# A product of spectra moved from VectorE to ScalarE and GpSimd, a bias given as an immediate, and two loads issued at other places

## The chip, the cores and the metric

The kernel runs on one core of a Trainium2 chip. The core has a matrix engine (TensorE, PE in the profile; its weight loads are shown apart as PEld), a vector engine (VectorE, DVE), an activation engine (ScalarE, ACT), a general engine (GpSimd, POOL) and a queue that only issues DMAs (SyncE, SP; ACT and POOL have DMA queues too). Each engine works its own instructions in order; semaphores make one wait for another. The matrix engine writes its results into PSUM, which GpSimd can't read in this kernel; everything else lies in SBUF, with DRAM behind it. The metric is the device time of one execution in microseconds (us); lower is better.

## The reference: what is computed

One input u of 2048 rows and 448 columns goes through two branches, and a gate per row mixes their outputs.

```python
g = _sigmoid((x * gate_w).sum(-1, keepdims=True))
a = _A_ref(x, ...)      # a long convolution
b = _B_ref(x, ...)      # attention in 4 segments with a memory
return g * a + (1 - g) * b
```

The convolution's filter is a sum of decaying oscillations, and the convolution is done by Fourier transforms of twice the length:

```python
P = jnp.exp((A * dt[:, None])[:, :, None] * pos[None, None, :])
K = 2.0 * jnp.einsum("dn,dnl->dl", C, P).real
Kf = jnp.fft.rfft(K, L2)
Uf = jnp.fft.rfft(u_t, L2)
y = jnp.fft.irfft(Uf * Kf[None, :, :], L2)[:, :, :L]
```

Its product `Uf * Kf` is the "product of spectra" of the title. The filter needs cosines and sines of 448 x 256 phases over the positions. The attention has 16 heads of 28 columns and 4 segments of 512 rows: within a segment a causal softmax, across segments a linear memory with a normalisation.

## The kernel before

The program has two halves.

The first half (to about 448 us) builds the filter, projects u to queries, keys and values, and does the first step of the Fourier transform of u. `first_half` goes through 56 steps n. In each, TensorE builds the phases in PSUM (`turns`), ScalarE makes from them, in `trig`, a sine straight from PSUM, an absolute value straight from PSUM, and a cosine in place in SBUF (a Sin with a bias of pi/2 and a negative scale), VectorE multiplies them with exponentials (`product`, lines 393 to 399), and TensorE sums them (`sums`). Between these steps `Feed` hands out pieces of the projections by a list of costs. In this half the order on VectorE and ScalarE is the program's own: `k.act`, `k.copy` and `k.vector` tie each instruction behind the one before it on its engine. The bias of the cosine is a tile of one column, `k.bhp`, filled once with pi/2; it is also the bias of one cosine in `prepare_params`.

The second half (`second_half`) holds the attention and the convolution. The attention works in 16 units (four segments times four groups of four heads). For each unit `maxima` does the scores of the row maxima (TensorE into `ps_a`, VectorE's masked maximum into `jk` and `mx`, line 992) and puts the negated maxima into the unit's query tile by a small DMA of POOL's queue (line 1004). `weigh` does the scores again with the maxima included, ScalarE takes the exponential into `PT` (line 1023), POOL masks it (line 1034). `values` multiplies with the values (`ps_pv`). At the end of a segment, `seg_end` normalises, recalls the memory and projects out; parts of that pass through DMAs of POOL's queue (lines 1067, 1068, 1098) and products on POOL (`skip`, line 1121).

The convolution (`convolve`) works in 32 chunks c. `transform` multiplies a chunk of the filter, `gk`, and ScalarE copies the result from PSUM into `ks` (line 599). `product` multiplies a chunk of u, `gu`, and VectorE multiplies the result in PSUM with `ks` into `pr` (line 604). `back` takes two finished chunks of `pr` through the first step back; ScalarE copies that into `bs` (line 617) and stores it. `pr` and `ks` have three buffers each. Each resumption of `convolve` does one of these steps; the loop over the units resumes it 1.15 times in each of the six rounds of a unit, from unit 1 to unit 12. At an odd c the order is: transform(c), product(c - 1), back(c - 3), which reads `pr` of c - 3 and c - 2.

The PSUM of the second half has three double banks of the tag `a`. The scores of both kinds, transform, product and back all take them in turn, so that an engine that is late to empty one holds TensorE. TensorE's own instructions are in program order (`k.mm`, `k.tr`). On ScalarE, VectorE and POOL in this half most instructions are placed by the planner of the framework, which orders what it can by its own estimates; the products of `skip` are held in program order.

Before the units start, `transform_k` does eight steps that turn the filter into `GK` in DRAM; each writes one store of 896 KB. In the same loop (`for r in range(8)`) the rounds of `maxima` of unit 0, and in the end the first of unit 1, are taken. Loads of a unit's q and k (`load`, 512 KB each, four buffers) are issued on SP's queue: unit 0 before the loop, unit 1 at r = 1, unit 2 after the loop and after the first loads of the convolution have been asked for, unit i + 3 at the start of unit i. SP's order is held by marks: `k.mark(x)` makes every later `k.dma` issue behind x. Each GK store is marked, and so is the load of k of the first three units. `k.ldma` also issues behind the latest load of a chunk of u (`k.late`); among the units' loads only unit 3 uses it.

Of the kernel before, what the change touches and what calls it, by code (L numbers as in the profile page):

```python
# [12 lines left out]
F32 = mybir.dt.float32  # L13
# [3 lines left out]
AF = mybir.ActivationFunctionType  # L17
ALU = mybir.AluOpType
# [5 lines left out]
D = 448  # L24
# [7 lines left out]
TWO_PI = 2 * math.pi  # L32
# [112 lines left out]
def accurate_exp(v, pool, x, P, W):  # L145


    def t(tag, dt=F32):
        return pool.tile([P, W], dt, tag=tag, name=tag)

    n, r, p = t("ee_n"), t("ee_r"), t("ee_p")
    a, b = t("ee_a"), t("ee_b")
    ia, ib = t("ee_ia", I32), t("ee_ib", I32)
    v.tensor_scalar(n, x, 1.0 / math.log(2.0), MAG, ALU.mult, ALU.add)
    v.tensor_scalar(n, n, MAG, -250.0, ALU.subtract, ALU.max)
    v.tensor_scalar(n, n, 250.0, None, ALU.min)
    c1 = 0.693359375
    c2 = math.log(2.0) - c1
    v.scalar_tensor_tensor(r, n, -c1, x, ALU.mult, ALU.add)
    v.scalar_tensor_tensor(r, n, -c2, r, ALU.mult, ALU.add)  # L160
    co = [1.0 / math.factorial(i) for i in range(9)]
    v.tensor_scalar(p, r, co[8], co[7], ALU.mult, ALU.add)
    for i in range(6, -1, -1):
        v.tensor_tensor(p, p, r, ALU.mult)
        v.tensor_scalar(p, p, co[i], None, ALU.add)
    v.tensor_scalar(a, n, 0.5, MAG, ALU.mult, ALU.add)
    v.tensor_scalar(a, a, MAG, None, ALU.subtract)
    v.tensor_tensor(b, n, a, ALU.subtract)
    for f, i in ((a, ia), (b, ib)):
        v.tensor_scalar(f, f, 127.0, 8388608.0, ALU.add, ALU.mult)  # L170
        v.tensor_copy(i, f)
    v.tensor_tensor(p, p, ia.bitcast(F32), ALU.mult)
    v.tensor_tensor(p, p, ib.bitcast(F32), ALU.mult)
    return p
# [3 lines left out]
def prepare_params(nc, k, pool, early, gp):  # L178

    ld = pool.tile([112, 4], F32, name="ld")
    nc.sync.dma_start(ld, k.log_dt.rearrange("(j p) -> p j", p=112))
    W = [112, 4, N]

    def new(nm, where=pool):
        return where.tile(W, F32, name="pin_" + nm)

    def load(nm, src, where=pool):
        t = new(nm, where)
        nc.sync.dma_start(t, src.rearrange("(j p) n -> p j n", p=112))
        return t

    cr = load("cr", k.C_real)
    ci = load("ci", k.C_imag)
    la = load("la", k.log_A_real)
    ai = load("ai", k.A_imag)
    k.ident = k.cp.tile([128, 128], F32, name="ident")  # L200
    nc.sync.dma_start(k.ident, k.c_id)
    k.ce = gp.tile([128, 3, 512], BF16, name="ce")
    nc.sync.dma_start(k.ce, k.c_ce)


    last = {}

    def chain(e, op, *args, **kw):
        if e in last:
            with k.issue_after(last[e].ins):  # L210
                x = op(*args, **kw)
        else:
            x = op(*args, **kw)
        last[e] = x

    class Chained:
        def __getattr__(self, name):
            return functools.partial(chain, "v", getattr(nc.vector, name))

    v = Chained()  # L220
    act = functools.partial(chain, "a", nc.scalar.activation)
    stt, tt, ts = v.scalar_tensor_tensor, v.tensor_tensor, v.tensor_scalar

    def wide(x):
        return x.unsqueeze(2).broadcast_to(W)

    def parts(w, t, sub, queue):
        for s in range(3):
            sp = pool.tile(W, BF16, tag="sp", name="sp", bufs=3)
            k.copy(sp, t, AF.Copy)  # L230
            if s < 2:
                sub(t, t, sp, ALU.subtract)
            queue(w[:, :, s], sp)
            yield

    b, c = new("b", early), new("c", early)
    mx, mn = new("mx", early), new("mn", early)
    f, g, e = (new(n, early) for n in "fge")
    a, d = new("a"), new("d")
    dt = accurate_exp(v, pool, ld, 112, 4)  # L240
    dtp = pool.tile([112, 4], F32, name="dtp")
    dt2 = pool.tile([112, 4], F32, name="dt2")

    act(b, cr, AF.Abs)
    act(c, ci, AF.Abs)
    act(la, la, AF.Exp)
    stt(mx, b, 1e-37, c, ALU.max, ALU.max)
    ts(dtp, dt, 1.0 / TWO_PI, None, ALU.mult)
    ts(dt2, dt, 2.0, None, ALU.mult)
    v.reciprocal(f, mx)  # L250
    yield 4
    nc.gpsimd.tensor_tensor(la, la, wide(dt), ALU.mult)
    for _ in parts(k.SD, la, nc.gpsimd.tensor_tensor, k.pdma):
        pass
    tt(mn, b, c, ALU.min)
    tt(f, f, mn, ALU.mult)
    act(g, f, AF.Arctan)
    yield 4
    yield "decays"
    tt(d, c, b, ALU.is_gt)  # L260

    tt(ai, ai, wide(dtp), ALU.mult)
    ts(e, ai, MAG, None, ALU.add)
    stt(a, e, MAG, ai, ALU.subtract, ALU.subtract)
    ts(d, d, 0.25, None, ALU.mult)

    stt(d, g, 1.0 / TWO_PI, d, ALU.mult, ALU.subtract)
    nc.scalar.activation(d, d, AF.Abs)
    ts(cr, cr, 0.0, 0.5, ALU.is_lt, ALU.mult)
    ts(ai, a, 32.0, None, ALU.mult)  # L270
    ts(e, ai, MAG, None, ALU.add)
    stt(ai, e, MAG, ai, ALU.subtract, ALU.subtract)
    tt(cr, d, cr, ALU.subtract)
    nc.scalar.activation(cr, cr, AF.Abs)
    stt(ai, a, 0.5, ai, ALU.mult, ALU.add)
    ts(ci, ci, 0.0, -2.0, ALU.is_lt, ALU.mult)
    ts(ci, ci, 1.0, None, ALU.add)
    yield 2
    tt(ci, cr, ci, ALU.mult)

    tt(ci, ci, ai, ALU.add)
    ts(e, ci, MAG, None, ALU.add)
    stt(d, e, MAG, ci, ALU.subtract, ALU.subtract)
    pa, pd = parts(k.SP[:, :, 0], a, tt, k.adma), parts(k.SP[:, :, 1], d, tt, k.adma)
    for s in range(3):
        for x in (pa, pd):
            next(x)
        yield 1
    act(c, g, AF.Sin, bias=k.bhp[:112], scale=-1.0)
    act(b, g, AF.Sin)  # L290
    yield "phases"
    yield 2
    tt(mx, mx, c, ALU.mult)
    tt(mn, mn, b, ALU.mult)
    tt(mx, mx, mn, ALU.add)
    tt(mx, mx, wide(dt2), ALU.mult)
    yield 4
    for nt in range(2):
        pt = k.ps("m")
        for j in range(4):  # L300
            k.tr(
                pt[:, 112 * j : 112 * j + 112], mx[:, j, 128 * nt : 128 * nt + 128], k.ident[:112, :112]
            )
        v.tensor_copy(
            k.cab[:, nt].rearrange("n (p j) -> n j p", j=4), pt[:, :D].rearrange("n (j p) -> n j p", j=4)
        )


def first_half(nc, k, gy, feed):
# [4 lines left out]
    act, v = k.act, nc.vector  # L314
# [61 lines left out]
    def trig(n):  # L376

        pt = arg.pop(n)
        cs[n] = t = gw.tile([128, 2, 2, 2, 256], F32, tag="cs", name="cs", bufs=2)
        pv = pt.rearrange("p t (w c) -> p t w c", w=2)  # L380
        act(t[:, 1].rearrange("p w t c -> p t w c"), pv, AF.Sin, scale=TWO_PI)
        act(t[:, 0].rearrange("p w t c -> p t w c"), pv, AF.Abs)
        fl = t[:, 0].rearrange("p w t c -> p (w t c)")
        act(fl, fl, AF.Sin, bias=k.bhp, scale=-TWO_PI)

    def product(n):
        J, c = divmod(n, 2)
# [179 lines left out]
def convolve(nc, k, fp):  # L567
# [3 lines left out]
    cf, cb, gk, gu, ks, pr = {}, {}, {}, {}, {}, {}  # L571
# [29 lines left out]
    def product(c):  # L601
        pt = second(c, gu.pop(c), 0)
        pr[c] = fp.tile([128, 2, D], F32, tag="pr", name="pr", bufs=3)
        nc.vector.tensor_tensor(pr[c], pt, ks.pop(c), ALU.mult)  # L604

    def back(c):

# [328 lines left out]
def attend(nc, k, ap):  # L936
# [15 lines left out]
    def load(i):  # L952
        if i >= 16:
            return
        s, hg = divmod(i, 4)
        queue = k.ldma if i == 3 else k.dma
        for t, T, src in (("q", Q, k.QD), ("k", K, k.KD)):
            T[i] = ap.tile([128, 2, SEG], F32R, tag=t, name=t + "u", bufs=4)
            x = queue(T[i].bitcast(F32), src[s, hg])
        if i < 3:  # L960
            k.mark(x)

# [242 lines left out]
def second_half(nc, k, ap, tp, fp, fin):  # L1205
# [5 lines left out]
    def step(g):  # L1211
        return next(g, none) is not none
# [16 lines left out]
    for r in range(8):  # L1229
        step(first)  # L1230
        if r == 1:
            k.load(1)
        for _ in range((0, 1, 2, 1, 2, 1, 1, 0)[r]):
            step(ms[0])
        if r >= 6:
            step(ms[1])
# [9 lines left out]
    fp = fp()  # L1246
    cv = convolve(nc, k, fp)
    step(cv)
    k.load(2)
    vals = k.values(0)  # L1250
    step(vals)
    for r in range(4):
# [72 lines left out]
def gated_mix(ctx, tc, k):  # L1325
    nc = tc.nc
# [14 lines left out]
    def act(*args, **kw):  # L1341
        if k.strict:
            return follow("act", nc.scalar.activation, *args, **kw)
        return tc.keep_in_program_order(nc.scalar.activation(*args, **kw))
# [124 lines left out]

    k.gates = gates  # L1470

    k.bhp = cp.tile([128, 1], F32, name="bhp")
    nc.vector.memset(k.bhp, math.pi / 2)

    def turn_over(pt, n):


# [134 lines left out]
```

## Time and profile before

| | |
|---|---|
| median of 3 runs | 866.55 us (866.17 to 876.26) |
| span of the profiled execution | 866.7 us |
| mean granted TensorE clock | 0.942 |
| busy: PE, PEld, DVE | 753.7, 410.3, 596.9 us |
| busy: ACT, POOL | 539.2, 173.1 us |
| DMA: moved, mean rate | 153.11 MB, 177 GB/s |

The profile is of one execution, whose span is the time from its first to its last instruction. Busy times count what an engine executes; PE's and PEld's overlap. Rows of a group read: line, engine, operation, output and inputs with their shapes, count, then the busy time in us and the mean of one in ns, and after the second bar the idle time of the engine just before these instructions, with what ended it. Rows of a timeline or of the chain begin with the start and the length in us. The clock is a share of full speed. Lines such as 1335, 1356, 1370, 1384 and 1386 are those of helpers (`follow`, `copy`, `mm`, `dma`), so tiles tell more than lines there.

### The profile page before, as it was taken

Reading aid. Unit: us, or ns where it says so; the run is one execution under the profiler, and the core shown is the slowest. Engines: PE = TensorE matmul, PEld = TensorE weight load, DVE = VectorE, ACT = ScalarE, POOL = GpSimd, SP = SyncE. Lnnn points to the kernel's source line nnn. Section 1 sums busy time; section 2 is a strip of 40 time slices with the busy share of each in tenths; the row PEclk is TensorE's granted clock in tenths of the full one; section 3 lists DMA queues with packets and bytes.
Section 4 is the critical chain, followed back from the end, with each engine's and each line's share of the span. In section 5 each row is a group of like instructions: output and inputs, shape, how many; then the busy total and the mean of one; then the engine's idle time right before and its main releaser. Section 6 shows DMA issues by size and latency. Waiting matters only on the chain.

```text
span 866.7 us, 18996 instructions
## 1 busy us (share of the span) xinstructions
PE 753.7 (87%) x7575; PEld 410.3 (47%) x7597; DVE 596.9 (69%) x1160; ACT 539.2 (62%) x638; POOL 173.1 (20%) x217
## 2 busy tenths in 40 slices
PE   1687988998879988799979799999997998888997
PEld 1364655765547644476534444444443443343443
DVE  7988778777787777877648656656664747664564
ACT  4876989798997999979842255544453434431220
POOL 5224111001110011101100111222313124222110
PEclk9998999998999999999979689999999999878799
DMA  9347753334633255323569948557465545654873
GB/s 242 91 110 247 227 185 104 96 111 154 205 124 96 96 169 194 122 92 132 178 218 347 317 133 264 178 193 249 139 222 189 193 162 168 216 187 164 221 231 100
DMA packets 88290, 153.11 MB, mean 177 GB/s; under 512 B 20626, under 2 KB 57162, under 8 KB 88154
## 3 DMA queue, kind: packets, MB, share of 16 engines
q1 hardware_dynamic: 79130, 140.83, 50.2%
q10 hardware_dynamic: 7424, 9.18, 3.1%
q0 software_dynamic: 1648, 1.89, 0.7%
q8 instruction: 60, 0.98, 0.5%
q14 instruction: 28, 0.23, 0.1%
HBM read 90.87 MB, written 60.63 MB: 175 GB/s over the span
## 4 chain that ended last, share of the span: by engine, by line
PE 52%; ACT 16%; DVE 13%; issue 7%; DMA 7%; POOL 2%; SPq 1%; ACTq 0%; DVEq 0%; POOLq 0%
PE ps_a L1370 18%; PE ps_m L1370 16%; PE ps_pv L1370 7%; ACT cs L1335 7%; PE ps_arg L1370 4%; DVE jk L992 3%; PE ps_k L1370 3%; PE ps_m L1373 2%; ACT L1335 2%; DVE Y L397 2%; DMA WD<-wsp 1%; ACT EX L1335 1%; DMA dn<-pvs 1%; DVE Y L398 1%; DMA ident<-in_c_id 1%
## 5 line engine op out<-in xcount | busy, mean ns | idle before, releaser
L1023 ACT ACTIVATE PT<-ps_a 128x1024 f32<-128x1024 f32 (+1 forms) x96 | 84.5, 881 | 122.9 <-PE ps_a L1370 115.9
L992 DVE CUSTOM_DVE_ANT_0 jk<-ps_a,mk 128x512 f32<-128x512 f32 (+3 forms) x256 | 124.9, 488 | 49.6 <-PE ps_a L1370 42.3
L359 POOL TENSOR_TENSOR EX<-EX,cab 128x1024 f32<-128x1024 f32 x28 | 54.0, 1928 | 309.3 <-ACT EX L1335 286.3
L1335 ACT ACTIVATE cs<-ps_arg 128x1024 f32<-128x1024 f32 x111 | 107.3, 1021 | 2.7 <-DVE Y L398 2.4
L1370 PE MATMUL ps_a<-qu,ku 32*128 32x512 f32 (+3 forms) x768 | 92.9, 364 | 1.3 <-DVE mx L992 0.6
L1370 PE MATMUL ps_m<-xh,w 112*128 112x512 f32 x256 | 92.9, 412 | 0.7 <-DVE lo L762 0.5
L393 DVE TENSOR_TENSOR X<-EX,cs 128x1024 f32<-128x1024 f32 x56 | 70.5, 1260 | 23.2 <-ACT cs L1335 21.5
L1034 POOL TENSOR_SCALAR_AFFINE_SELECT PT<-PT 128x256 f32<-128x256 f32 (+1 forms) x96 | 47.1, 493 | 178.9 <-ACT PT L1023 178.7
L1370 PE MATMUL ps_k<-Y,X 128*32 128x64 f32 x3584 | 64.1, 226 | 11.8 <-DVE Y L398 11.8
L1370 PEld LDWEIGHTS ps_k<-Y,X 128*32 128x32 f32 x3584 | 54.9, 113 | 38.0 <-DVE Y L398 19.9
L397 DVE TENSOR_TENSOR Y<-EY,cs 128x1024 f32<-128x1024 f32 x56 | 70.0, 1251 | 0.0
L1370 PEld LDWEIGHTS ps_a<-qu,ku 32*128 32x128 f32 x768 | 64.8, 201 | 10.1 <-issue 3.2
L1335 ACT ACTIVATE cs<-cs,bhp 128x1024 f32<-128x1024 f32 x56 | 64.5, 1151 | 1.8
L1370 PE MATMUL ps_a<-ku,qu 32*128 32x512 f32 (+3 forms) x256 | 47.2, 404 | 16.0 <-DVE mx L992 8.4
L399 DVE SCALAR_TENSOR_TENSOR Y<-EY,cs 128x512 f32<-128x512 f32 x56 | 39.4, 704 | 30.5 <-ACT cs L1335 29.7
L1335 ACT ACTIVATE EY<-ps_arg 128x1024 f32<-128x1024 f32 x52 | 53.1, 1030 | 11.1 <-PE ps_arg L1370 10.0
L1370 PEld LDWEIGHTS ps_m<-xh,w 112*128 112x128 f32 x256 | 48.0, 188 | 20.0 <-issue 7.6
L1370 PEld LDWEIGHTS ps_a<-ku,qu 32*128 32x128 f32 x256 | 23.1, 195 | 62.7 <-issue 28.6
L1370 PE MATMUL ps_m<-xl,w 112*128 112x512 f32 x128 | 50.3, 393 | 0.0
L1370 PE MATMUL ps_arg<-ct,lh 64*128 64x512 bf16 x224 | 43.1, 386 | 8.1 <-ACT cs L1335 5.0
L1370 PEld LDWEIGHTS <-lh 64*128 64x128 bf16 x392 | 22.1, 95 | 50.6 <-issue 37.8
L604 DVE TENSOR_TENSOR pr<-ps_a,ks 128x896 f32<-128x896 f32 x32 | 34.7, 1085 | 15.7 <-PE ps_a L1370 15.4
(214 smaller groups left out, 1408.7 us busy)
## 6 DMA issues: line engine op xcount, KB each, us to landing
w<-WD SPq DMA_DIRECT2D x32, 448.0 KB
qu<-QD SPq DMA_DIRECT2D x16, 512.0 KB
ku<-KD SPq DMA_DIRECT2D x16, 512.0 KB
GU<-gs SPq DMA_DIRECT2D x32, 224.0 KB
GK<-gs SPq DMA_DIRECT2D x8, 896.0 KB
gk<-GK SPq DMA_DIRECT2D x32, 224.0 KB
gu<-GU SPq DMA_DIRECT2D x32, 224.0 KB
BB<-bs ACTq DMA_DIRECT2D x16, 448.0 KB
```

What stands on the lines that cost most here:

```text
L359: nc.gpsimd.tensor_tensor(o, o, cab, ALU.mult)
L393: v.tensor_tensor(X, ex, t[:, :, 0], ALU.mult)
L397: v.tensor_tensor(Y[:, :, :, :32], lo, y[:, :, :, ::-1], ALU.mult)
L398: v.tensor_tensor(Y[:, 0, :, 32:], ey[:, :, 32:], y[:, 0], ALU.mult)
L399: v.scalar_tensor_tensor(Y[:, 1, :, 32:], ey[:, :, 32:], -1.0, y[:, 1], ALU.mult, ALU.mult)
L604: nc.vector.tensor_tensor(pr[c], pt, ks.pop(c), ALU.mult)
L992: v.tensor_tensor_reduce(junk[:, :n], pt[:, x, o : o + n], k.mk[:, SEG - n :], 1.0, -3e38, ALU.add, ALU.max, mx[:, 3 - t, h : h + 1],)
L1023: nc.scalar.activation(PT[:, 2 * hp : 2 * hp + 2, 512 * b : 512 * b + n], pt[:, :, :n], AF.Exp, scale=SCALE)
L1034: nc.gpsimd.affine_select(sl, sl, pat, ALU.is_ge, 0.0, base=0, channel_multiplier=-1)
L1335: x = op(*args, **kw)
L1370: tc.keep_in_program_order(nc.tensor.matmul(*args, **kw))
L1373: tc.keep_in_program_order(nc.tensor.transpose(*args))
```

## The change

There are three parts.

1. In `convolve`'s `product`, VectorE's multiplication of PSUM with `ks` goes. ScalarE copies the result from PSUM into a new tile `us`, which has one buffer, and POOL multiplies `us` with `ks` into `pr`.
2. The cosine's bias is given as a number in the instruction, in `trig` and in `prepare_params`, and the tile `bhp` with its memset goes.
3. Unit 2's load is issued in the loop of eight steps, at r = 3, rather than after it; and unit 3's load uses the same queue function as the others, without the wait for the latest load of a chunk of u. The load of k of unit 2 is still marked, so the GK stores of the later steps issue behind it.

```diff
@@ prepare_params
-    act(c, g, AF.Sin, bias=k.bhp[:112], scale=-1.0)
+    act(c, g, AF.Sin, bias=math.pi / 2, scale=-1.0)
@@ first_half, trig
-        act(fl, fl, AF.Sin, bias=k.bhp, scale=-TWO_PI)
+        act(fl, fl, AF.Sin, bias=math.pi / 2, scale=-TWO_PI)
@@ convolve, product
         pr[c] = fp.tile([128, 2, D], F32, tag="pr", name="pr", bufs=3)
-        nc.vector.tensor_tensor(pr[c], pt, ks.pop(c), ALU.mult)
+        us = fp.tile([128, 2, D], F32, tag="us", name="us", bufs=1)
+        nc.scalar.activation(us, pt, AF.Copy)
+        nc.gpsimd.tensor_tensor(pr[c], us, ks.pop(c), ALU.mult)
@@ attend, load
         s, hg = divmod(i, 4)
-        queue = k.ldma if i == 3 else k.dma
         for t, T, src in (("q", Q, k.QD), ("k", K, k.KD)):
             T[i] = ap.tile([128, 2, SEG], F32R, tag=t, name=t + "u", bufs=4)
-            x = queue(T[i].bitcast(F32), src[s, hg])
+            x = k.dma(T[i].bitcast(F32), src[s, hg])
         if i < 3:
             k.mark(x)
@@ second_half, the loop of eight steps
         if r == 1:
             k.load(1)
+        if r == 3:
+            k.load(2)
@@ second_half, after it
     step(cv)
-    k.load(2)
     vals = k.values(0)
@@ gated_mix
-    k.bhp = cp.tile([128, 1], F32, name="bhp")
-    nc.vector.memset(k.bhp, math.pi / 2)
```

## The prediction

> **What bounds the kernel now.** I began with the windows by stage: four stretches, with the busy time of each engine (the count of instructions behind it), the granted TensorE clock, the DMA share and GB/s. Then comes the page's chain of work that ended last.
>
> ```profile
> 0.00:448.00 448.00, 377.58 (x5124) 239.25 (x5128) 343.85 (x478) 378.29 (x441) 82.63 (x63) 0.97 0.47 150
> 448.00:498.00 50.00, 41.97 (x253) 21.20 (x254) 32.88 (x105) 13.66 (x16) 5.49 (x9) 0.81 0.90 326
> 498.00:770.00 272.00, 249.84 (x1763) 112.31 (x1778) 167.39 (x489) 127.24 (x155) 69.34 (x120) 0.95 0.57 187
> ...
> PE 52%; ACT 16%; DVE 13%; issue 7%; DMA 7%; POOL 2%; SPq 1%; ACTq 0%; DVEq 0%; POOLq 0%
> ```
>
> The columns of a window are PE, PEld, DVE, ACT, POOL. The change touches one thing in each stretch. In the first (to 448 us) PE and ACT are level at 378 us: neither is the bound alone, they take turns. In the second (448 to 498) the DMA engines are 0.90 busy and PE is at a clock of 0.81. In the third (498 to 770, which holds the convolution) PE is 249.84 of 272 us busy, and the others are far from full. There PE can gain at most the 22.2 us in which it is idle, and what the clock loses.
>
> Next the second stretch in order of time, since PE waits there on the load that is moved. The first row is from the chain, the others from the timelines of SP, DVE and PE.
>
> ```profile
> 476.73 6.66 DMA ku<-KD
> ...
> 458.64 16.62 SPq L1386 DMA_DIRECT2D GK<-gs  x6
> 475.32 0.42 SPq L1386 DMA_DIRECT2D qu<-QD  x1
> 476.73 0.71 SPq L1386 DMA_DIRECT2D ku<-KD  x1
> ...
> 480.16 0.08 DVE L992 DVE_READ_ACCUMULATOR2_ANT mx<- 128x1 f32 x1
> 481.90 0.42 DVE L992 CUSTOM_DVE_ANT_0 jk<-ps_a,mk 128x256 f32<-128x256 f32 x1
> 484.35 0.69 DVE L992 CUSTOM_DVE_ANT_0 jk<-ps_a,mk 128x512 f32<-128x512 f32 x1 [2.02 <-PE ps_a L1370]
> ...
> 483.52 0.79 PE L1370 MATMUL ps_a<-ku,qu 32*128 32x512 f32 x2 [4.47 <-DMA ku<-KD]
> ```
>
> Unit 2's q and k are issued behind the last GK store and land 6.66 us later; PE stands still for 4.47 us, so it had stopped at 479.05. How the clock takes such a gap:
>
> ```profile
> 478.00:480.00 2.00, 1.05 (x5) 0.30 (x5) 1.75 (x9) 0.00 (x0) 0.00 (x0) 1.00 0.94 275
> ...
> 482.00:484.00 2.00, 0.48 (x4) 0.51 (x6) 0.33 (x2) 0.00 (x0) 0.00 (x0) 0.68 1.05 407
> ...
> 506.00:508.00 2.00, 2.00 (x30) 0.90 (x22) 0.00 (x0) 0.48 (x1) 0.00 (x0) 0.84 0.03 8
> 568.00:570.00 2.00, 0.90 (x4) 0.21 (x3) 1.89 (x10) 0.17 (x1) 0.75 (x1) 1.00 0.84 272
> 570.00:572.00 2.00, 1.59 (x12) 0.72 (x12) 1.75 (x5) 0.60 (x1) 0.69 (x2) 0.87 0.18 68
> ...
> 608.00:610.00 2.00, 1.20 (x19) 0.98 (x17) 1.48 (x3) 1.71 (x2) 0.84 (x2) 1.00 0.03 8
> ...
> 484.30:498.70 14.40, 13.60 (x77) 8.01 (x73) 8.57 (x33) 5.76 (x7) 2.83 (x6) 0.50 0.85 293
> 498.70:507.40 8.70, 8.70 (x51) 3.33 (x52) 2.80 (x8) 2.99 (x4) 1.45 (x3) 0.54 0.44 149
> ```
>
> The clock falls to 0.50 after the gap and stays there until about 507. It also falls around 571, where the 2 us before held 0.90 us of PE work; it holds at 608, with 1.20 us.
>
> **The load of unit 2.** It moves ahead of GK's last four stores. Those six GK issues run from 458.64 to 475.26, some 3.3 us apart, so the load is issued near 464 rather than 475.32 and 476.73. Even with another 6.66 us to land it is there by 472, well before PE needs it at 479. The wait goes, and the next late thing is DVE: PE's slot in PSUM (ps_a has three) comes free when the reductions of unit 1 end, the first at 480.24 (480.16 + 0.08), the last at 482.32. So PE starts at about 480.3 in place of 483.52: 3.2 us saved. From below, 2.0 us is what DVE was idle before 484.35. If the clock also stayed full, 13.60 + 8.70 us of PE work at half clock would shrink; that is the first rival.
>
> Which is likelier? From 479.05 to 482.3 PE would have only unit 2's first step and unit 0's first step to run, about 1.5 us at full clock (0.79 + 1.65 at half is some 2.4): under half of the time, nearer to the 0.90 of 2 us at 568 than to the 1.20 of 2 us at 608. I take it that the clock falls: 3.2 us.
>
> The Trainium skill, "TensorE: Matmul & The Clock Gate", Part 1, has the clock fall after at least one idle window of about 3.4 us; by that rule the remaining gap of 1.2 us would leave it full, and the sum would be that of the first rival, 852.1. The rows at 568 to 572 differ: there it fell without such a gap.
>
> What the move costs: 1 MB goes ahead of four GK stores (896 KB each), 2.6 us at the 407 GB/s of the row at 482. GK's four buffers and the gk loads behind take it up, since the bytes ahead of those loads are the same in sum; if that cover is gone, the cost is 2.6 us. On SP's queue two issues (0.42 and 0.71 us) stand ahead of four GK stores that are 3.3 us apart: nothing. Unit 3 no longer waits for the latest gu load; its 1 MB may pass the gk and gu loads of the first chunks, which the convolution reads after 498. I cost it at nothing, at most 2.6 us.
>
> **The cosine's bias.** Rows of ACT, then the chain's shares in the window to 448 us:
>
> ```profile
> L1335 ACT ACTIVATE cs<-cs,bhp 128x1024 f32<-128x1024 f32 x56 | 64.5, 1151 | 1.8
> L1335 ACT ACTIVATE cs<-ps_arg 128x1024 f32<-128x1024 f32 x111 | 107.3, 1021 | 2.7 <-DVE Y L398 2.4 <-PE ps_arg L1370 0.2
> L211 ACT ACTIVATE pin_c<-pin_g,bhp 112x1024 f32<-112x1024 f32 x1 | 1.1, 1148 | 0.0
> L211 ACT ACTIVATE pin_b<-pin_g 112x1024 f32<-112x1024 f32 x1 | 1.0, 1040 | 0.0
> ...
> by line: PE ps_m L1370 21.6%; ACT cs L1335 13.6%; PE ps_arg L1370 8.0%; issue 7.5%; PE ps_k L1370 6.0%; ACT L1335 4.0%; DVE Y L397 3.4%; PE ps_m L1373 2.9%; DMA WD<-wsp 2.4%; ACT EX L1335 2.3%; DVE Y L398 2.1%; DMA ident<-in_c_id 1.7%; DVE
> ```
>
> The third and fourth rows are the same Sin on the same shape, with the bias tile and without: 1148 against 1040 ns, so 0.108 us each, 56 x 0.108 = 6.0 us of ACT. On the chain lie 13.6% of 448 = 60.9 us of these operations' 171.8 us, or 35%: 2.2 us saved. Bounds: 0 (PE and DVE take the turn over) and 6.0. The memset of bhp (one small DVE instruction at the start) is nothing.
>
> **The product.** Rows of the groups, of what PE and POOL wait for from 498 to 770, of DVE and POOL around 733, and of PE around the first products:
>
> ```profile
> L604 DVE TENSOR_TENSOR pr<-ps_a,ks 128x896 f32<-128x896 f32 x32 | 34.7, 1085 | 15.7 <-PE ps_a L1370 15.4 <-ACT PT L1023 0.4
> L599 ACT ACTIVATE ks<-ps_a 128x896 f32<-128x896 f32 x32 | 29.3, 917 | 14.1 <-PE ps_a L1370 13.5 <-PE ps_pv L1370 0.5
> L359 POOL TENSOR_TENSOR EX<-EX,cab 128x1024 f32<-128x1024 f32 x28 | 54.0, 1928 | 309.3 <-ACT EX L1335 286.3 <-DVE cab L211 22.9
> L1121 POOL TENSOR_TENSOR xt<-xt,dbc 128x448 f32<-128x448 f32 x16 | 18.3, 1157 | 23.0 <-DMA xt<-in_A_u 19.6 <-issue 3.4
> ...
> PE ps_a L1370 <- DVE mx L992: 8.8, 12, 2.9
> PE ps_a L1370 <- DVE pr L604: 7.0, 8, 4.4
> ...
> POOL xt L1121 <- DMA xt<-in_A_u: 19.6, 5, 7.5
> POOL RD L1067 <- DVE rs L1065: 17.0, 4, 5.5
> ...
> 733.02 4.33 DVE L1136 TENSOR_SCALAR xt<-xt,gt 128x448 f32<-128x448 f32 x2 [0.19 <-POOL xt L1121]
> 738.27 0.44 DVE L1136 TENSOR_SCALAR xt<-xt,gt 128x448 f32<-128x448 f32 x1
> ...
> 731.85 4.39 POOL L1121 TENSOR_TENSOR xt<-xt,dbc 128x448 f32<-128x448 f32 x4
> ...
> 514.59 1.02 PE L1370 MATMUL ps_a<-gu,cf 64*128 64x448 f32 x4
> 519.90 0.60 PE L1370 MATMUL ps_a<-pr,cb 128*64 128x448 f32 x2
> ```
>
> DVE loses 34.7 us. ACT gains 32 copies like ks: 29.3 us. POOL gains 32 products of 896 columns: between the rows of 448 and 1024, 1157 + 0.78 x 771 = 1757 ns, so 56.2 us. Then DVE has 132.7, ACT 156.6 and POOL 125.6 of 272 us: none becomes the bound by its sum. What counts is PE's waits. On pr it waits 7.0 us; the longest, 4.4, is one wait where pr stood behind DVE's work on xt (4.33 us for two that take 0.44 each alone), which ended only after the four xt on POOL (731.85 + 4.39); on POOL pr stands behind the same four, so that wait stays. The other 2.6 us are seven short waits for a slot, which ACT's copy (0.917 against 1.085) gives back a little sooner: I take half, 1.3 us. Below, a loss: see the second rival; above, all of the 7.0 and 8.8.
>
> The path to back grows: from the end of gu's matmul at 515.61 to the matmul on pr at 519.90 are 4.3 us; 0.92 + 1.76 and two handovers take 2.8. 1.5 us is the cover. New waits: us has one buffer, so ACT's next copy waits for POOL's product, and behind that copy stand ACT's exponentials, which free ps_a; products spaced by 5 us and more hide that. The product may also stand behind a POOL instruction that itself waits.
>
> Those rows at 733 also show DVE held while POOL reads SBUF. POOL's share in reading grows by 56.2 us, 21% of the stretch, so DVE instructions like L1136 are held more often, by up to 1.76 us each. DVE has 34.7 us to give for that: nothing on the path, at most what the second rival has.
>
> The path to back grows: from the end of gu's matmul at 515.61 to the matmul on pr at 519.90 are 4.3 us; 0.92 + 1.76 and two handovers take 2.8. 1.5 us is the cover. New waits: us has one buffer, so ACT's next copy waits for POOL's product, and behind that copy stand ACT's exponentials, which free ps_a; products spaced by 5 us and more hide that. The product may also stand behind a POOL instruction that itself waits.
>
> Those rows at 733 also show DVE held while POOL reads SBUF. POOL's share in reading grows by 56.2 us, 21% of the stretch, so DVE instructions like L1136 are held more often, by up to 1.76 us each. DVE has 34.7 us to give for that: nothing on the path, at most what the second rival has. The Trainium skill, "SBUF — State Buffer", "Who interferes with whom", says that DVE's two-port modes, and its instructions with two SBUF inputs, contend with GpSimd for the shared ports; the row at 733 agrees (4.33 us against 2 x 0.44), and the rule speaks against this part of the change.
>
> The sum: 866.7 - 3.2 - 2.2 - 1.3 = 860.0. The span of 866.7 us stands 0.15 above the median of 866.55, so nothing is corrected.
>
> **The rivals.**
>
> The clock stays full near 480. Then 14.40 us shrink to DVE's 8.57 at best, and 8.70 us, scaled by the 13.60 that PE would do in about 8.4, to 5.4: with DVE's 2.0 that is 11.1 us in place of 3.2, 852.1 us. For it: PE would not stand still for more than 1.2 us at once. Against it: the rows at 568.
>
> Slower: POOL's queue holds the product back. The two waits quoted are 36.6 us in nine waits, mean 4.1. A product queued behind a whole one comes 4.1 - 1.5 = 2.6 us late, PE stops, and each stop can cost 2 us more at half clock (as at 571). Nine of them make 41 us. It turns the result slower than 866.7 at two, and slower by 2% at six: six give 860.0 + 27.6 = 888. Against it: mostly a product falls outside these waits (36.6 of 272 us), or ahead of them in the queue.
>
> DVE was the true limit: with 34.7 us less, PE's waits on mx and pr go altogether: 15.8 in place of 1.3, 845.5 us. Against it: most of mx's waits follow DVE's waits for DMA or POOL, not pr.
>
> The change does nothing: the DMA engines are full, GK pays what unit 2 gains, and ACT's 6 us are hidden: 865.
>
> **How the numbers follow.** Forecast 0.40 (own range 856 to 865); clock full 0.25; POOL's queue 0.17 (868 to 895); DVE the limit 0.13; nothing 0.05. 860 is the likeliest. 846 to 878 cuts half of the DVE case and half of the POOL case: 0.15 left out. A measurement of this kernel tells about 2% from no change, so 849.2 and 883.9 are the bounds. Faster: the DVE case and a third of the clock case, 0.21. Slower: half of the POOL case, 0.09. Same: 0.70.
>
> **What would show it.** PE's wait on ku near 480 is gone and its first row there starts by 481; the clock after 483 tells forecast from first rival. The cosine takes 1.04 us. pr is a row of POOL near 1.76 us, us one of ACT near 0.92, and PE's matmuls on pr and gk wait on ACT or POOL for no more than a few us in all. I am wrong if PE waits for POOL by tens of us, if unit 2 still lands after 479, or if the order of ACT or POOL was laid out anew, so that exponentials come late.

## The result, and the profile after

| | before | after |
|---|---|---|
| median, 20 runs each, same chip | 867.68 us | 860.94 us |
| lowest to highest | 856.81 to 876.26 | 852.61 to 868.45 |
| span of the profiled execution | 866.7 us | 856.8 us |

The ratio is 0.992, with a 95% interval of 0.9897 to 0.9944: 0.8% faster, which is 6.7 us between the medians. The two profiled executions are 9.9 us apart. One execution differs from the next by several us in either kernel, so some 3 of those 9.9 us are not the change.

First the busy time of the page of after, then its groups of instructions, with the forms kept apart (busy time in us and mean ns after the bar).

```profile
PE 751.5 (88%) x7597; PEld 406.7 (47%) x7597; DVE 567.1 (66%) x1127; ACT 561.7 (66%) x670; POOL 240.4 (28%) x249
```

```profile
L1337 ACT ACTIVATE cs<-cs 128x1024 f32<-128x1024 f32 x56 | 59.3, 1059 | 1.8
L605 ACT ACTIVATE us<-ps_a 128x896 f32<-128x896 f32 x32 | 29.4, 918 | 10.5 <-PE ps_a L1372 9.4 <-POOL PT L1035 0.7 <-PE ps_pv L1372 0.2
L606 POOL TENSOR_TENSOR pr<-us,ks 128x896 f32<-128x896 f32 x32 | 67.2, 2101 | 24.2 <-ACT us L605 24.0
```

Work moved as the diff says: VectorE is busy for 29.8 us less than before, POOL for 67.3 more, ScalarE for 22.5 more (29.4 of copies, less 92 ns in each of 56 cosines, would be 24.2; where two instructions overlap, the busy time counts them once). TensorE is busy for as long as before (751.5 and 753.7 us). The cosine now takes 1059 ns and not 1151; the product takes 2101 ns on POOL.

What PE and POOL of after waited for between 498 and 770 us, in the view of waits (us in total, times, longest):

```profile
PE ps_a L1372 <- DVE mx L993: 9.1, 6, 3.7
PE ps_a L1372 <- POOL pr L606: 2.6, 1, 2.6
...
POOL pr L606 <- ACT us L605: 24.0, 21, 4.0
```

PE's waits on pr were 7.0 us in eight; one of 2.6 is left. The waits on mx are what they were (8.8 before). POOL mostly waits for ScalarE's copy and not the other way round, so POOL has room.

Now the stretch in which units 0 to 2 start: rows of PE that began after a wait, then SP's issues of the two moved loads, from the timelines of after.

```profile
450.86 0.50 PE L1372 MATMUL ps_a<-ku,qu 32*128 32x512 f32 x2 [2.23 <-DMA ku<-KD]
...
480.39 0.49 PE L1372 MATMUL ps_a<-ku,qu 32*128 32x512 f32 x2 [1.27 <-DVE mx L993]
481.43 0.96 PE L1372 MATMUL ps_a<-qu,ku 32*128 32x512 f32 x6 [0.55 <-DVE mx L993]
...
484.06 1.64 PE L1372 MATMUL ps_a<-qu,ku 32*128 32x512 f32 x6 [1.08 <-DVE mx L993]
```

```profile
460.47 0.90 SPq L1388 DMA_DIRECT2D ku<-KD  x1
464.23 11.13 SPq L1388 DMA_DIRECT2D GK<-gs  x4
...
477.67 0.55 SPq L1388 DMA_DIRECT2D ku<-KD  x1
```

Unit 2's k is issued at 460.47 in place of 476.73, ahead of the last four GK stores, and the wait of 4.47 us on it is gone: PE goes on at 480.39, held 1.27 us by VectorE's maxima. But three short waits stand within 5 us, and the clock follows. Windows of after (PE, PEld, DVE, ACT, POOL, then clock, DMA share, GB/s):

```profile
0.00:448.00 448.00, 378.62 (x5158) 238.34 (x5160) 346.59 (x478) 374.06 (x444) 84.16 (x65) 0.98 0.49 153
448.00:498.00 50.00, 42.70 (x232) 21.32 (x228) 33.41 (x109) 12.75 (x15) 4.07 (x8) 0.71 0.83 306
498.00:770.00 272.00, 253.23 (x1818) 113.83 (x1815) 140.11 (x462) 157.39 (x189) 138.44 (x155) 0.96 0.61 198
...
456.00:468.00 12.00, 10.96 (x54) 5.62 (x48) 6.66 (x26) 2.16 (x3) 0.00 (x0) 0.50 0.87 323
482.00:484.00 2.00, 0.89 (x6) 0.18 (x2) 1.82 (x6) 1.02 (x1) 0.40 (x1) 0.76 1.04 422
484.00:508.00 24.00, 23.74 (x125) 11.54 (x125) 10.15 (x38) 8.91 (x11) 3.88 (x8) 0.52 0.56 193
```

From 484 to 508 PE is busy for 23.74 of 24 us, at a clock of 0.52. A busy share of 99% looks like a bound engine; the clock beside it says that it does half of what it could. The same happens from 456 to 468, behind unit 0's wait of 2.23 us on its own k at 450.86, which the profile of before does not have: there the clock in 448 to 498 was 0.81, here it is 0.71. The fall comes some 5 us after that wait.

So in the profiles the change loses in this stretch and gains ahead of it and behind it. Three marks divide the span: the end of the last copy into kb on VectorE (the first half's end), and the starts of ScalarE's mn of units 0, 2, 3 and so on, one for each unit. The first two rows of after:

```profile
442.93 1.00 DVE L420 COPY kb<-ps_k 128x512 f32<-128x512 f32 x1
```

```profile
471.34 0.59 ACT L1003 ACTIVATE mn<-ps_m 4x512 fp32r<-4x512 f32 x1 [0.27 <-PE ps_m L1375]
```

The stages so cut, in us, for the profiled executions of before and after:

| stage | before | after |
|---|---|---|
| first half, to kb's end | 447.98 | 443.93 |
| kb's end to mn of unit 0 | 23.26 | 27.41 |
| mn 0 to mn 2 | 36.77 | 35.87 |
| mn 2 to mn 3 | 17.37 | 17.37 |
| mn 3 to mn 15 (the convolution lies in it) | 285.55 | 276.49 |
| mn 15 to the end | 55.77 | 55.73 |

### The profile page after: what moved, and what is told of

Read it like the earlier page. It is cut to its first block, busy times and chain, and to the rows that moved or that the text cites. A ratio compares the mean times of both kernels' runs of the same rounds, so it can differ in the third digit from the quotient of the medians.

```text
span 856.8 us, 19037 instructions
## 1 busy us (share of the span) xinstructions
PE 751.5 (88%) x7597; PEld 406.7 (47%) x7597; DVE 567.1 (66%) x1127; ACT 561.7 (66%) x670; POOL 240.4 (28%) x249
## 4 chain that ended last, share of the span: by engine, by line
PE 51%; DVE 16%; ACT 15%; DMA 7%; issue 7%; POOL 2%; SPq 1%; ACTq 0%; DVEq 0%; POOLq 0%
PE ps_a L1372 19%; PE ps_m L1372 17%; PE ps_pv L1372 7%; ACT cs L1337 6%; PE ps_k L1372 3%; PE ps_arg L1372 3%; DVE Y L397 3%; DVE jk L993 3%; DVE X L393 2%; ACT L1337 2%; DVE Y L398 2%; PE ps_m L1375 2%; DMA w<-WD 1%; ACT EX L1337 1%; DMA dn<-pvs 1%
## 5 line engine op out<-in xcount | busy, mean ns | idle before, releaser
L359 POOL TENSOR_TENSOR EX<-EX,cab 128x1024 f32<-128x1024 f32 x28 | 54.0, 1928 | 307.7 <-ACT EX L1337 284.6
L606 POOL TENSOR_TENSOR pr<-us,ks 128x896 f32<-128x896 f32 x32 | 67.2, 2101 | 24.2 <-ACT us L605 24.0
L1372 PEld LDWEIGHTS ps_k<-Y,X 128*32 128x32 f32 x3584 | 54.9, 113 | 39.2 <-DVE Y L398 22.5
L1337 ACT ACTIVATE cs<-cs 128x1024 f32<-128x1024 f32 x56 | 59.3, 1059 | 1.8
```

The costliest lines, as they stand in the source:

```text
L359: nc.gpsimd.tensor_tensor(o, o, cab, ALU.mult)
L606: nc.gpsimd.tensor_tensor(pr[c], us, ks.pop(c), ALU.mult)
L1372: tc.keep_in_program_order(nc.tensor.matmul(*args, **kw))
```

## The experiments

Twelve kernels, in three groups of four; each group ran on one chip, a different one for each, beside the kernel before. All stages below are cut as above. The ratios and intervals are those on record; they are not the quotients of the medians in the tables, and the two can differ by some tenths of a percent.

### Each part alone, and all but the loads

The bias alone (the same is done in `prepare_params`, and `bhp` goes):

```diff
-        act(fl, fl, AF.Sin, bias=k.bhp, scale=-TWO_PI)
+        act(fl, fl, AF.Sin, bias=math.pi / 2, scale=-TWO_PI)
```

> Only the bias as an immediate, against the kernel before (about 867 us). Theory A, the steps of the prediction: the cosine falls from 1151 to about 1059 ns, the first half ends 2 to 4 us earlier and the whole is 2.2 us shorter. Theory B, from the trace after the change: the first half ends 4 us earlier, but the second half then starts into a TensorE that waits for unit 0's loads, the clock falls near 455 us, and what is left at the end is under 1 us. Either way ACT's cosines sum to 59 us in place of 64.5.

The product alone:

```diff
-        nc.vector.tensor_tensor(pr[c], pt, ks.pop(c), ALU.mult)
+        us = fp.tile([128, 2, D], F32, tag="us", name="us", bufs=1)
+        nc.scalar.activation(us, pt, AF.Copy)
+        nc.gpsimd.tensor_tensor(pr[c], us, ks.pop(c), ALU.mult)
```

> Only the product as a copy on ScalarE and a product on GpSimd. Theory A: 1.3 us shorter. Theory B: this part carries the gain, because VectorE's maxima come sooner in the stretch from 500 to 770 us: 5 to 9 us shorter, with TensorE's waits on pr (7.0 us before) nearly gone. pr takes 2.1 us on GpSimd in both.

The two loads alone:

```diff
-        queue = k.ldma if i == 3 else k.dma
...
-            x = queue(T[i].bitcast(F32), src[s, hg])
+            x = k.dma(T[i].bitcast(F32), src[s, hg])
...
+        if r == 3:
+            k.load(2)
...
-    k.load(2)
```

> Only the loads of units 2 and 3 moved. Theory A: 3.2 us shorter, TensorE's wait of 4.5 us on ku near 480 gone, the clock still at half until about 507. Theory B: the wait goes but its place is taken by VectorE's maxima and the clock at half speed, and 0 to 2 us are left. If the clock stays full after 483, 8 to 11 us shorter.

Bias and product together, that is the whole change without its third part (the first two diffs):

> Bias and product changed, the loads as before. Theory A: 3.5 us shorter than before, so 3.2 slower than the whole change. Theory B: 5 to 7 us shorter than before, within 2 us of the whole change (861).

| kernel | median us | ratio to before | 95% interval |
|---|---|---|---|
| bias | 865.96 | 0.9989 | 0.9963 to 1.0016 |
| product | 868.27 | 0.9995 | 0.9963 to 1.0027 |
| loads | 866.78 | 0.9968 | 0.9928 to 1.0008 |
| bias and product | 864.52 | 0.9931 | 0.9900 to 0.9963 |
| before, beside them | 870.47 | | |

Each part alone is within its measurement of nothing; the first two together are 0.7% faster. The theory that the product alone carries 5 to 9 us falls: its interval ends at -0.4%. Beyond that, parts of 1 to 4 us drown here in a spread of 10 us and more between executions. For the bias the figures differ most: its median is 4.5 us below that of the kernel before, while its ratio has 1.0 us, and at most 3.2. Its profile goes as theory B has it (the first half ends at 443.19 us, PE then waits 2.49 us on unit 0's k, and the clock falls behind that), but neither theory is excluded; nor is either of the two for the loads, or for bias and product together. So the second group holds the clock, and the parts are then read from stages and not from totals.

What the four profiles agree on: with unit 2's load early, the stage from mn 0 to mn 1 is 15.34 us, in the loads' kernel as in after; without, it is 17.2 to 17.7. And the wait on unit 2's k near 480 is still there without it, as here in the kernel of bias and product:

```profile
480.89 0.79 PE L1372 MATMUL ps_a<-ku,qu 32*128 32x512 f32 x2 [4.64 <-DMA ku<-KD]
```

But the loads' kernel takes 31.41 us from kb's end to mn 0, before 23.26. Is that the price of the early load? The next group asks.

### The clock held by added matmuls, and the load of unit 3 alone

The kernel has a helper that issues matmuls on a constant tile. The first kernel of this group is the changed one with more of them at two places; the second has those of the first place alone, the third those of the second.

```diff
+        turn_over((0, 10, 3, 3, 3, 3, 0, 0)[r])
         for _ in range((0, 1, 2, 1, 2, 1, 1, 0)[r]):
             step(ms[0])
...
-            if r in WARM:
+            if i == 0 and r < 3:
+                turn_over(4)
+            elif r in WARM:
                 turn_over(WARM[r])
```

Both places:

> The changed kernel with extra matmuls on a constant tile (the kernel's own turn_over), put ahead of unit 0's maxima in the loop that transforms k (10, 3, 3, 3, 3 of them in rounds 1 to 5) and 4 ahead of each of the first three steps of unit 0's weights. They fill TensorE's short waits near 450 and 480 to 486. Theory A (the half clock that follows these waits, 456 to 469 and 484 to 507 us in the changed kernel's profile, is caused by them and costs time): the granted clock stays at 1.00 in both stretches, the stage from the end of kb's copy to unit 0's minimum falls from 27.4 to about 22, the stage from unit 0's to unit 1's stays or falls, the two after it fall by 3 to 5 together; 848 to 854 us against the changed kernel's 861, a ratio to the kernel before of 0.98. Theory B (VectorE's 0.7-us maxima are what the stage waits for, and the added matmuls only add 25 x 0.22 to 0.5 us on TensorE): clock full, stages shorter by less than 1 us or longer, 860 to 866 us. Theory C (the clock falls whatever is filled): 0.50 in the same places, added matmuls cost 0.4 us each, 866 to 872 us.

The loop that transforms k alone:

> The same with the extra matmuls in the loop that transforms k alone. Theory A: the clock stays full from 450 to 480, the stage to unit 0's minimum falls from 27.4 to about 22; the fall near 484 is still there; 855 to 857 us. Theory B: 860 to 863 us with the clock full. Theory C: clock 0.50 from 456 as before, 866 us.

Unit 0's steps alone:

> The same with the extra matmuls in unit 0's first three steps alone. Theory A: the clock stays full from 480 to 510, stages from unit 0's minimum to unit 2's fall by 3 to 6 us; 855 to 858 us. Theory B: clock full and 860 to 863 us. Theory C: clock 0.50 from 484 as before, 863 to 866 us.

And the changed kernel with unit 2's load back where it was, so that only unit 3's moves:

```diff
-        if r == 3:
-            k.load(2)
...
+    k.load(2)
```

> The changed kernel with unit 2's load back behind the convolution's first loads; unit 3's load stays on the queue of the ordinary transfers. Theory A (unit 2's early load removes the wait of 4.5 us near 480, and pays for it in the loop that transforms k, where its 460.0 issue crowds the stores and unit 1's load): the wait on ku near 480 is back, unit 0's minimum to unit 1's is 17.3 us again instead of 15.3, and the stage from kb's copy to unit 0's minimum is 24 to 25 us instead of 27.4; 860 to 862 us, the same as the changed kernel. Theory B (the longer stage there is unit 0's own load or chance): unit 0's minimum comes after 27 us here too, and the time is 2 us above the changed kernel's, 863.

| kernel | median us | ratio to before | 95% interval |
|---|---|---|---|
| after, both places | 855.19 | 0.9835 | 0.9796 to 0.9874 |
| after, first place | 864.76 | 0.9930 | 0.9892 to 0.9967 |
| after, second place | 858.69 | 0.9900 | 0.9847 to 0.9953 |
| after, unit 2's load back | 863.19 | 0.9933 | 0.9904 to 0.9962 |
| before, beside them | 868.38 | | |

With matmuls added at both places the kernel beats the kernel before and the changed one; its interval lies wholly below that of the changed kernel (0.9897 to 0.9944). The windows of that kernel, for the same times as above:

```profile
448.00:498.00 50.00, 46.16 (x332) 22.27 (x334) 36.90 (x118) 17.80 (x22) 5.45 (x11) 1.00 0.87 317
456.00:468.00 12.00, 11.82 (x86) 5.36 (x83) 8.95 (x28) 4.14 (x5) 0.00 (x0) 1.00 0.92 322
482.00:484.00 2.00, 2.00 (x21) 1.30 (x21) 1.31 (x4) 1.07 (x3) 0.78 (x2) 1.00 1.06 385
484.00:508.00 24.00, 22.26 (x183) 11.09 (x184) 14.53 (x59) 15.89 (x20) 10.20 (x15) 1.00 0.60 206
```

The clock is full in each; in 484 to 508 PE does 183 matmuls in place of 125 and is busy for less time. From kb's end to mn 2 this kernel takes 25.67 + 28.26 = 53.9 us, after 27.41 + 35.87 = 63.3. Most of that is behind mn 0: the stage ahead of it was expected to fall to about 22 and did not. That VectorE's maxima set the pace there, and that added matmuls only cost time, has fallen; so has the idea that the clock falls whatever is filled.

The first place alone is worth nothing that these runs can tell: its clock is 1.00 from 448 to 480 and falls near 481, as expected, but the 855 to 857 us did not come. The second alone is not told from the changed kernel either (the intervals overlap). Only both together are shown to be faster than the changed kernel. In the second place's profile the clock is 1.00 in both stretches: there PE's wait near 450 was 1.22 us, ended by VectorE's copy gs and not by unit 0's k, and no fall followed. Its stage to mn 0 took 21.71 us, some 4 us less than in the kernel with both places: where the clock holds by itself, the 22 matmuls of the first place seem to cost that much, by these two profiles.

The kernel with unit 2's load back shows both waits on ku:

```profile
455.11 0.50 PE L1371 MATMUL ps_a<-ku,qu 32*128 32x512 f32 x2 [2.44 <-DMA ku<-KD]
...
487.97 0.79 PE L1371 MATMUL ps_a<-ku,qu 32*128 32x512 f32 x2 [4.58 <-DMA ku<-KD]
```

Its stage to mn 0 is 27.61 us, as long as after's 27.41, without the early load, and the second place's kernel has 21.71 with it. So the early load is not what makes after's long; a wait of over 2 us on unit 0's own k comes early in that stage in both. In before's profile PE does not wait on that load. The kernels of the bias and of bias and product have such a wait too (2.49 and 2.03 us), with stages of 25.03 and 24.56 us, so the wait alone does not set the length. What makes that load late in some executions was not tried.

### Each part taken out where the clock is held

The third group starts from the kernel with both places filled and takes one part of the change out of it, with the diffs of the first group reversed; the last is the kernel before with the added matmuls and nothing else.

Without the product's part:

> The changed kernel with the extra matmuls at both places and the product back on VectorE, so that the product is tried where the clock does not fall at 456 or 484. Against the 855.2 us of the kernel with the extra matmuls and the whole change: theory A (the product shortens the stages between unit 4's and unit 7's minimum by some 3.5 us, which the single-part runs could not resolve beside their spread) 858 to 859 us, the three stages 18.3, 21.9 and 24.7 again; theory B (the product by itself is worth nothing to the end, as its single-part run had it) 855 us.

Without the bias:

> The same with the product on GpSimd and the cosine's bias a tensor again. Theory A (the bias is worth 4 us in the first half, by the single part's profile): 859 us, the first half 446 to 448 instead of 442 to 444. Theory B (the first half's end varies from execution to execution by as much, and the bias is worth the 2.2 us of the forecast or less): 855 to 857 us.

Without the loads:

> The same with product and bias, and the loads of units 2 and 3 where they were. Theory A (the load of unit 2 comes late by 4 to 5 us near 480, longer than the extra matmuls there fill, and the clock falls behind it as in the kernel before): the wait on ku near 480 is back, clock 0.50 from 484 to 505, unit 0's minimum to unit 2's 36 us instead of 28; 862 to 864 us. Theory B (the extra matmuls cover that too): 857 us, clock full.

The kernel before with the added matmuls:

> The kernel before with the extra matmuls and nothing of the change. Theory A (the extra matmuls are worth little without the early load of unit 2, since its wait near 480 is longer than they fill): 867 to 869 us, the same as the kernel before. Theory B (they give their 5 to 6 us here too): 862 us.

| kernel, matmuls added at both places | median us | ratio to before | 95% interval |
|---|---|---|---|
| whole change (group above) | 855.19 | 0.9835 | 0.9796 to 0.9874 |
| without the product | 859.31 | 0.9866 | 0.9820 to 0.9912 |
| without the bias | 860.90 | 0.9889 | 0.9841 to 0.9937 |
| without the loads | 857.88 | 0.9870 | 0.9824 to 0.9915 |
| without any of it | 867.03 | 0.9982 | 0.9956 to 1.0008 |
| before, beside the last four | 868.73 | | |

Every part taken out brings the median up, by 2.7 to 5.7 us, though the whole ran on another chip and each interval still overlaps its own. Added to the kernel before, with none of the change, the matmuls bring 1.7 us between the medians, which its interval does not tell from nothing. The time is the one expected, but the reason given for it does not fit the profile: from kb's end to mn 2 this kernel takes 55.19 us where before takes 60.03, and its first half ended 4.7 us later (452.70).

Without the product, the stages from mn 4 to mn 7 were expected at 18.3, 21.9 and 24.7 us, some 3.5 us longer in sum than with it. They are 18.33, 21.07 and 24.64, against 17.40, 20.84 and 24.06 in the whole: 1.7 us. From mn 3 to mn 15 these two profiles are level (279.65 and 279.73). So this pair shows half of the gain in the stages expected, and none of it by mn 15.

The loads' part was expected to leave a clock of 0.50 from 484 to 505. That expectation failed:

```profile
484.91 0.50 PE L1375 MATMUL ps_a<-ku,qu 32*128 32x512 f32 x2 [2.48 <-DMA ku<-KD]
```

```profile
486.00:490.00 4.00, 4.00 (x18) 1.73 (x19) 2.24 (x8) 2.13 (x3) 0.41 (x2) 0.57 1.06 387
490.00:508.00 18.00, 16.97 (x156) 9.34 (x154) 11.53 (x43) 10.51 (x13) 5.05 (x11) 1.00 0.70 253
```

The added matmuls fill half of the wait, the clock falls for some 3 us, and is full again at 490. The stage from mn 0 to mn 2 is 30.04 us in this kernel and in the one without any of the change, and 28.26 in the two with the early load and a full clock (the whole change, and that without the product). From kb's end to mn 2, so that the stage ahead is in it, the four give 55.18 and 55.19 against 53.93 and 53.96: 1.2 us is the early load worth where matmuls are added.

The kernel without the bias is the odd one: its clock is full up to 492 and then 0.50, with the same matmuls in it.

```profile
490.87 1.08 PE L1375 MATMUL ps_a<-qu,ku 32*128 32x384 f32 x12 [0.88 <-DVE mx L993]
```

```profile
490.00:492.00 2.00, 1.13 (x13) 1.05 (x14) 1.75 (x9) 0.32 (x2) 0.40 (x1) 1.00 1.06 347
492.00:494.00 2.00, 2.00 (x12) 0.95 (x11) 1.20 (x9) 1.08 (x2) 0.41 (x1) 0.58 0.94 274
494.00:506.00 12.00, 11.86 (x63) 4.64 (x61) 4.05 (x14) 4.08 (x5) 2.09 (x4) 0.50 0.42 151
```

The kernel with the whole change has the same wait, 0.87 us, at its matmul of the same form at 485.13, and keeps its clock. Its stage from mn 0 to mn 2 is 28.26 us, the other's 33.57: 5.3 us for one fall, behind one and the same wait. The second place's kernel and the one without the product have that wait too (0.87 and 0.86 us), and keep their clock. So part of the 5.7 us between these two kernels is that fall and not the bias, and for the bias the first half has to be read by itself.

## Why the prediction was right, step by step

The time was right: 860.0 forecast, 860.94 measured, a gain of 6.7 forecast and 6.7 measured. Its terms were not all right, so the agreement is partly luck. To size them, the stages of 13 profiled executions are compared (the two kernels and the twelve experiments, less that of the first place alone, whose profiled execution took 870.1 us where its median is 864.8). The plus-minus is the standard error of the difference of two means, from the spread within each group.

**The load of unit 2: mechanism right, size too large (3.2 us taken, about 1 read).** The wait on ku is gone, PE goes on at 480.39 (forecast 480.3), the clock falls all the same and stays down to 507, all as forecast. Counted from mn 0, PE starts unit 2 after 9.05 us, where it was 12.28: the 3.2 us are there. But mn 1 comes only 1.9 us earlier (15.34 after 17.22), and since PE waits for maxima again and runs at half clock, mn 1 to mn 2 grows by 1.0 us (19.55 to 20.53). Mn 0 to mn 2 gives 0.9 us in the two profiles, and 1.2 us is what the four kernels with added matmuls show. The forecast took PE's earlier start as saved to the end; about a third of it was, by these. The loads alone, 0.9968 (0.9928 to 1.0008), exclude neither 3.2 nor 1.2.

**The cosine's bias: right in kind, size uncertain (2.2 us taken, about 4 read).** 92 ns were saved on each and not 108: the pair in prepare_params, one instruction each on 112 partitions, was taken for the cosine's. The Trainium skill, "ScalarE: Activation LUTs", section "What ACT_TABLE_LOAD costs", has about 93 ns for each operand given by a pointer, which agrees. Of the 5.2 us that this makes, the forecast put 35% on the path, by the chain's shares (35% of its 6.0 is 2.1, not 2.2). The first half ends at 448.65 us on average in the five profiles with the bias a tensor, and at 444.58 in the eight with the number: 4.1 us earlier, plus-minus 1.4. The stretch from the first to the last cosine tells the same, without what follows them. From the view of the tile cs, of the product's kernel and of the bias's (ns least, median and most, first and last start):

```profile
L1337 ACT ACTIVATE cs<-cs,bhp x56: 1147/1152/1160, 61.3 to 436.6; 128x1024 f32<-128x1024 f32 x56
```

```profile
L1335 ACT ACTIVATE cs<-cs x56: 1056/1060/1067, 61.2 to 431.2; 128x1024 f32<-128x1024 f32 x56
```

From first to last start it is 375.3 us against 370.0; over the five and the eight profiles, 374.4 against 370.8, plus-minus 1.1. So most of what ScalarE saves seems to reach the end of the first half, and not a third; that an operation absent from the chain at some places still carries the delay of the one that stands in it there would explain it, and was not tried. With the profile of the first place alone put in too, the 4.1 would be 3.7; and 2.2 lies less than one and a half plus-minus from any of these. The ratio of the bias alone has 1.0 us, and at most 3.2, for the whole program. So the size of this term stays open between some 1 and 4 us.

**The product: right in kind, its duration mis-sized, its gain perhaps.** 2101 ns stand against the 1757 taken. The step that failed is the interpolation between POOL's xt (1157 ns for 448 columns) and EX (1928 for 1024): they take other operands, and EX takes 1.88 ns a column where xt takes 2.58. EX's second factor, cab, is one value repeated over 32 columns (line 359), while the product, like xt, reads two full tiles. In proportion to xt, 896 columns are 2314 ns; the measured 2.34 ns a column lies nearer to that row. Whether the repetition makes EX the quicker was not tried. The Trainium skill, "GPSIMD Engine Reference", section 3.1, has about 2.6 cycles an element for two inputs; at its 1.2 GHz the estimate is 1941 ns without the dispatch, which agrees better with the 2101 measured than the interpolation did. It cost little, since PE waited only once on pr, 2.6 us. The gain taken was 1.3 us; mn 3 to mn 15 takes 283.54 us in the five profiles with the product on VectorE and 280.30 in the eight with it on POOL: 3.2 us, plus-minus 1.7, which does not tell it from 1.3. In mn 4 to mn 11 alone the difference is 3.6, plus-minus 0.7 (158.09 to 154.52); behind that it is lost in the noise. With the profile of the first place alone put in too, these would be 2.3 and 3.1. Two of those stages differ alike in every profile: mn 4 to mn 5 takes 18.33 to 18.35 us with VectorE and 17.40 to 17.43 with POOL, mn 6 to mn 7 24.64 to 24.66 and 24.05 to 24.08. That makes 1.5 us.

The waits on pr went from 7.0 to 2.6 us, and the one long wait that was to stay did not. The forecast had it stay because pr would stand behind POOL's four xt. In the profile of after, POOL works one product (726.37) ahead of its four xt (728.43) and the next (734.96) behind them, and PE waits for neither. The forecast also had VectorE's work on xt held more often beside a busier POOL, by up to 1.76 us each. The longest of the four became shorter, 1.3 us after 3.8, in all profiles with the product on POOL. From the views of the tile xt, of before and of after:

```profile
L1136 DVE TENSOR_SCALAR xt<-xt,gt x4: 437/514/3818, 733.0 to 739.1; 128x448 f32<-128x448 f32 x4
```

```profile
L1137 DVE TENSOR_SCALAR xt<-xt,gt x4: 521/948/1322, 729.6 to 733.3; 128x448 f32<-128x448 f32 x4
```

By these sizes the sum is 1.2 + 4.1 + 3.2 = 8.5 us, within the measured interval (0.56% to 1.03%, or 4.9 to 8.9 us). The plus-minus of the last two together is some 2.2 us, so this sum is no better than the 6.7 as a figure for the whole. It says that one term was too large and that two were rather too small, and that the three together met the measured gain by luck.

**The rivals.** The clock did not stay full: the row at 484 to 508 decides for the forecast. What a full clock would be worth was priced at 852.1 us; the kernel that holds it came to 855.2, from another cause than forecast: the gaps were filled, not too short. The Trainium skill's rule, "TensorE: Matmul & The Clock Gate", Part 1 (a fall after an idle window of about 3.4 us), does not fit these rows: no wait of after near 480 is longer than 1.27 us. POOL's queue did hold the product back, once, as this rival describes it: the product of the last chunk stood behind two DMAs that waited themselves, and began at 753.14 though its us was there at 749.98. From the timelines of ACT, POOL and PE of after:

```profile
749.06 0.92 ACT L605 ACTIVATE us<-ps_a 128x896 f32<-128x896 f32 x1
...
750.19 0.75 POOL L1068 DMA_DIRECT2D RD<-rs  x1 [2.73 <-DVE rs L1066]
...
752.59 0.53 POOL L1069 DMA_DIRECT2D r<-RD  x1 [1.22 <-DMA RD<-rs]
753.14 2.08 POOL L606 TENSOR_TENSOR pr<-us,ks 128x896 f32<-128x896 f32 x1
...
755.28 0.97 PE L1372 MATMUL ps_a<-pr,cb 128*64 128x448 f32 x4 [2.55 <-POOL pr L606]
```

PE waited 2.55 us, where the rival has 2.6 for one such stop, and the clock fell behind it, as the rival has it too (0.53 from 756 to 758, 0.50 from 758 to 762). By its own prices it needed two of them to be slower than before, and there was one. VectorE was not the limit: waits on mx are 9.1 us after 8.8. That the change does nothing is excluded by the interval.

## What to carry to other kernels

Read the clock beside the busy share: a PE that is 99% busy at 0.52 is not the bound it looks, and such a stretch can be won by filling the short waits ahead of it. Here matmuls on a constant tile brought 5.7 us between the medians on top of the change, and 1.7, not told from nothing, without it. Where one execution differs from the next by more than an edit is worth, cut the span into stages at fixed instructions and pool the profiles of all kernels that share a stage, and give the error with it: that showed the bias's gain in the first half, 4.1 us, plus-minus 1.4, where a dozen timings of the single edit told nothing, and it also shows that the size is not settled. And price an operation by a row with the same kinds of operands, not by the nearest size.

## What the runs showed of the hardware

- The clock fell within or behind waits from 0.88 us (the kernel without the bias) to 4.95 us (the bias alone, near 480), and not behind one of 1.65 us (the product alone, at 456.10). A wait of 0.86 to 0.88 us at the same matmuls stands in four kernels with matmuls added in unit 0's steps; the clock fell behind it in one and not in three. Which of such waits brings a fall was not settled.
- Once down it stayed at half for some 23 us with PE 99% busy in the changed kernel (484 to 507). It stayed down for some 3 us in the kernel without the loads (486 to 490), where more matmuls of 128 x 128 with 512 columns stood in between, but for some 14 us in the kernel without the bias (492 to 506), where the added ones stood ahead of the fall. The Trainium skill, "TensorE: Matmul & The Clock Gate", Part 1, has the full clock back after about 3.4 us of sustained work; the 3 us agree, the 23 and 14 do not. What counts as work there no run here tells.
- A bias given as a tile costs ScalarE 92 ns more than a number, at 128 x 1024 (1151 and 1059 ns). A product of two tiles of 128 x 896 takes POOL 2101 ns from SBUF, and took VectorE 1085 ns with one operand in PSUM.
- A program's first half, the same instructions on the same data, ended between 441.8 and 448.5 us in the eight profiles with the bias a number. That spread is as large as the gain of the whole change, and it is made ahead of all that the loads and the product touch.
